# Transposing k and q of ten units by DMA in 16-bit words instead of by TensorE

## The chip, the cores and the metric

The kernel runs on one core of a Trainium2 chip. The metric is the device time of one execution in microseconds, lower being better. The kernel before takes 637.39 us (median of three runs, 636.07 to 639.22). The profile is of one execution with a span of 637.1 us.

## The reference

A linear attention with decay (a "retention") feeds a two-layer network with a SiLU between its layers. Batch 4, 8 heads, 768 positions, head size 64, model width 512, hidden width 2048; all is computed to 32-bit accuracy.

```python
gamma = 1.0 - 2.0 ** (-5.0 - np.arange(H))
for t in range(S):
    state = gamma * state + outer(k[:, :, t], v[:, :, t])     # per batch and head, 64 x 64
    y[:, :, t] = scale * (q[:, :, t] @ state)
x = y.transpose(0, 2, 1, 3).reshape(B * S, H * D)             # 3072 x 512
h = x @ w_in                                                  # 512 -> 2048
g = h * (1.0 / (1.0 + np.exp(-h)))
out = g @ w_out                                               # 2048 -> 512
```

## The kernel before

**Units and visits.** The sequence is cut into 6 chunks of 128 positions. A unit is one chunk of one of the 4 batches, so there are 24 units, numbered chunk by chunk. Inside a chunk the recurrence is written as a masked product of q and k (the scores) plus a product of q with the carried state. A function `visit(m)` advances three units by one stage each: unit m is staged (k and q transposed), unit m - 1 gets its state products and its scores, and unit m - 2 gets its output y.

The scores need k and q with the head dimension on the partitions, but they lie in memory with the position there. `stage_t` (L353) transposes them: four TensorE transposes of 128x128 for k and four for q (L360), each group into one bank of PSUM, and a ScalarE copy of 128x512 for each into the tiles `kt` and `qt` (L362). `stage_s` (L370) uses k untransposed, already scaled by `scale_k` (L330), for the state products; `stage_a` uses `kt` and `qt` for the scores.

**The two layers.** `product_in(c, f)` (L535) is one step of the first layer: chunk c of all four batches (512 rows) by one block f of 128 hidden columns. Each operand is split into a high and a low part, so the step has twelve matmuls of 128x512, eight into the bank `ha` and four into `hb` (L539). ScalarE copies `ha` out (L543), VectorE subtracts `hb` (L547), ScalarE applies SiLU (L551), and one step later SyncE stores the result, g, in DRAM (L557). Three PSUM banks are shared by `ha` and `hb` in turn (`turn`, L317); in the kernel before, the transposed k of a visit takes one turn as well. The tile for g has three buffers. The second layer (L665 on) reads g back and starts near 370 us, when the first is done.

**What sets the order.** The order on TensorE is as written. The main loop (L645) runs through the steps and, behind some of them, a visit: unit 14 behind step (1, 15), units 15 to 17 behind (2, 9), (2, 11), (2, 13), units 18 to 21 behind (3, 1), (3, 5), (3, 9), (3, 13), units 22 and 23 behind (4, 1) and (4, 5). Two further visits, behind (4, 9) and (4, 13), stage nothing and finish the last two units. So visits are two steps apart in chunk 2 and four steps apart later. On the other engines a scheduler orders what is ready, in the order of the program where it can choose. Lists (`behind_copy`, `behind_next`) hold work back until the copy of `ha` or the subtraction of a coming step has been issued.

**Queues.** Nearly all transfers are issued by SyncE, in order: an issue that waits holds up all behind it. Transfers use eight completion semaphores in turn, so an issue may also have to wait for the one eight before it. Loads of k and q for unit m + 2 are issued at the end of visit m (L528), of v for m + 1. Beside them SyncE issues the stores of g, and loads of the weights (`wf`), which VectorE and ScalarE convert from 64-bit words (L172); the converted second-layer weights are stored again (`wod`, L238). The tiles `kf`, `qf` and `vf` have three, two and three buffers.

Of the kernel before, what the change touches and what calls it, by code (L numbers as in the profile page):

```python
# [12 lines left out]
FP32 = mybir.dt.float32  # L13
FP32R = mybir.dt.float32r
U32 = mybir.dt.uint32
AF = mybir.ActivationFunctionType
ALU = mybir.AluOpType

# [13 lines left out]
def kernel(  # L32
# [6 lines left out]
    moe_w_out: bass.AP,  # L39
    out: bass.AP,  # L40
):

# [17 lines left out]
    nc = tc.nc  # L60
    B, H, S, D = q.shape
    DM, DF = moe_w_in.shape
    C = 128
    NC = S // C
    HP = H // 2
# [15 lines left out]
    dram = pool("dram", 1, space=bass.MemoryType.DRAM)  # L81
# [3 lines left out]
    ld = pool("ld", 2)  # L85
    one = pool("one", 1)
# [24 lines left out]
    def split_w(f, w32, name, factor, to):  # L111
# [4 lines left out]
        with tc.issue_after(held[0] if f >= NF - 4 else evac[0]):  # L116
            nc.scalar.activation(out=w[:, 0, :], in_=w32, func=AF.Copy, scale=HALF * factor)
        high = w[:, 0, :].bitcast(FP32)
        yield
        nc.vector.scalar_tensor_tensor(out=lo, in0=w32, scalar=factor, in1=high,  # L120
                                       op0=ALU.mult, op1=ALU.subtract)
        nc.scalar.activation(out=w[:, 1, :], in_=lo, func=AF.Copy, scale=1.0 / EPS)
        nc.vector.scalar_tensor_tensor(out=w[:, 2, :], in0=high, scalar=EPS, in1=lo,
# [3 lines left out]
    units = [(c, b) for c in range(NC) for b in range(B)]  # L127
    kqv = {"k": {}, "q": {}, "v": {}}
    EARLY = 2 * B
    early = {}  # L130

    def load(name, n):
        if n >= len(units):
            return
        c, b = units[n]
        src = {"k": k, "q": q, "v": v}[name]
        if n < EARLY:

            if n not in early:
                early[n] = wpool.tile([128, 3, H, D], FP32, tag=f"w{4 + n}", name=f"kqv_{n}")  # L140
            t = early[n][:, "kqv".index(name)]
        else:
            t = ld.tile([128, H, D], FP32, tag=f"{name}f", name=f"{name}f_{n}",
                        bufs=2 if name == "q" else 3)
        nc.sync.dma_start(out=t, in_=src[b, :, ds(c * C, C)].rearrange("h t d -> t h d"))  # L145
        kqv[name][n] = t
# [6 lines left out]
    def load_w(i):  # L153
        if i >= 2 * NF:
            return
        if wide:
            t = stage.tile([128, 2 * DM], U32, tag="wf", name=f"wf_{i}")
            w_in, w_out, n = moe_w_in.bitcast(U32), moe_w_out.bitcast(U32), 256
        else:
# [12 lines left out]
    def convert_w(i):  # L172
# [130 lines left out]
    xt, kt, qt, am = {}, {}, {}, {}  # L303
    behind_next, behind_mask, behind_copy = [], [], []
# [25 lines left out]
    def scale_k(n):  # L330
        if 0 <= n < len(units):
            t = kqv["k"][n]
            if units[n][0] == NC - 1:
                t = t[:D]
            if 2 * B <= n < 3 * B + 2:

                def half(heads):
                    for h in heads:
                        nc.scalar.activation(out=t[:, h, :], in_=t[:, h, :], func=AF.Copy,
                                             scale=gk[:, units[n][0], h : h + 1])  # L340

                half(range(H // 2))
                behind_copy.append(lambda: half(range(H // 2, H)))
                return
            g = gk[: t.shape[0], units[n][0], :].unsqueeze(2).to_broadcast([t.shape[0], H, D])
            nc.vector.tensor_tensor(out=t, in0=t, in1=g, op=ALU.mult)

    def scale_q(n):
        c, b = units[n]
        t, g = (x if c > 0 else x[:, :, D:] for x in (qt[n], gq))  # L350
        nc.vector.tensor_tensor(out=t, in0=t, in1=g, op=ALU.mult)

    def stage_t(n):  # L353

        for name, to, bufs, src, tp in (
                ("kt", kt, 2, kqv["k"][n], turn(f"kp_{n}")),
                ("qt", qt, 3, kqv["q"].pop(n), banks("q", f"qp_{n}", 1)[:, 0])):
            tp = tp.rearrange("p (a t) -> p a t", a=HP)
            for a in range(HP):
                nc.tensor.transpose(tp[:, a, :], src[:, 2 * a : 2 * a + 2, :], ident)  # L360
            to[n] = one.tile([128, HP, C], FP32, tag=name, name=f"{name}_{n}", bufs=bufs)
            evac[:] = [nc.scalar.copy(out=to[n], in_=tp).ins]  # L362
# [128 lines left out]
    def late_x(b):  # L491
        if b == 0:
            xt[LATE] = xpool.tile([128, 3, KIN, NT], FP32R, tag="xt", name=f"xt_{LATE}")
        with tc.issue_after(copied[0]), tc.issue_after(taken_out[0]):
            split_x(LATE, b, None, y_late.pop(b))

    def visit(m):

        first, mid, last = (0 <= m - i < len(units) for i in range(3))
        if first:  # L500
            stage_t(m)
        if last:
            scores, states_with, yp = stage_y(m - 2)
            scores()
        if mid:
            sc, sums = score_tile(m - 1)
            stage_s(m - 1, sums)
        if last:
            states_with(0)
        if mid:  # L510
            stage_a(m - 1, sc)
            if m > 1 and units[m - 1][1] == 0:
                next_chunk()
            with tc.issue_after(taken_out[0]) if taken_out else ExitStack():
                finish_a(m - 1, sc, sums)
            with tc.issue_after(masked[0]):
                while behind_mask:
                    list(behind_mask.pop(0))
            scale_q(m - 1)
        if m == 0:  # L520
            chunk_decays()
            first_chunk()
        if first:
            scale_k(m)
        if last:
            states_with(1)
            finish_y(m - 2, yp)
        for name, n in (("k", m + 2), ("q", m + 2), ("v", m + 1)):  # L528
            if n >= EARLY:
                load(name, n)  # L530


    pending = []

    def product_in(c, f):  # L535
        ha, hb = turn(f"ha_{c}_{f}"), turn(f"hb_{c}_{f}")
        for i in range(3):
            for kk in range(KIN):
                nc.tensor.matmul(hb if i == 2 else ha, lhsT=w_sb[f][:, i, ts(kk, 128)],  # L539
                                 rhs=xt[c][:, i, kk, :], start=kk == 0 and i != 1,  # L540
                                 stop=kk == KIN - 1 and i != 0)
        hs = hpool.tile([128, NT], FP32, tag="hs", name=f"g_{c}_{f}")
        copied[:] = [nc.scalar.activation(out=hs, in_=ha, func=AF.Copy, scale=ONE_E).ins]  # L543
        with tc.issue_after(copied[0]):
            while behind_copy:
                behind_copy.pop(0)()
        taken_out[:] = [nc.vector.tensor_tensor(out=hs, in0=hs, in1=hb, op=ALU.subtract).ins]  # L547
        with tc.issue_after(taken_out[0]):
            while behind_next:
                behind_next.pop(0)()  # L550
        nc.scalar.activation(out=hs, in_=hs, func=AF.Silu)  # L551
        pending.append((c, f, hs))

    def put_g(keep):
        while len(pending) > keep:
            c, f, g = pending.pop(0)
            nc.sync.dma_start(out=g_dram[c, f], in_=g)  # L557
# [50 lines left out]
    for m in range(EARLY + 2):  # L608
# [9 lines left out]
        elif m == EARLY:  # L618
# [11 lines left out]
    steps = pairs + three + rest + last + groups  # L630
# [6 lines left out]
    at = ([(1, NF - 1)] + [(2, f) for f in range(NF - 7, NF - 2, 2)] +  # L637
          [(c, 4 * i + 1) for c in range(3, NC - 1) for i in range(B)])
# [3 lines left out]
    behind[1, NF - 4] = lambda: [late_x(0), late_y(2), late_x(1), late_y(3)]  # L642
    behind[1, NF - 2] = lambda: late_x(2)
    behind[1, NF - 1] = lambda: [late_x(3), visit(EARLY + 6)]
    for n, (c, f) in enumerate(steps):  # L645
        product_in(c, f)
        if (c, f) in takes:
            take_w(taken_out[0], 2 if n < len(pairs) else int(n < len(pairs + three)))
        put_g(1)
        behind.get((c, f), lambda: None)()  # L650
        if c == NC - 1:
            if f == 0:
                get_w(0)
                get_w(1)
            if f < NF - 4:
                w_out(f)
            if f >= NF - 6:
                if f == NF - 6:
                    for n in range(G_AHEAD):
                        get(n)  # L660
                if f >= NF - S_AHEAD:
                    split(f - NF + S_AHEAD)
    put_g(0)

    for c in range(NC):  # L665
# [8 lines left out]
        for f in range(NF):  # L674
            n = c * NF + f
# [3 lines left out]
            t = ready.pop(n)  # L679
# [9 lines left out]
        for b in range(B):  # L689
            oa, ob = acc[b]  # L690
            o = one.tile([128, DM], FP32, tag=("kt", "qt")[b % 2], name=f"o_{c}_{b}",
                         bufs=(2, 3)[b % 2])
            rows = ds(b * S + c * C, C)
# [7 lines left out]
            n = 2 if b == B - 1 else 1  # L701
# [36 lines left out]
```

## Time and profile before

| | |
|---|---|
| time, median of 3 | 637.39 us |
| TensorE busy, matmuls | 613.2 us (96%) |
| VectorE busy | 421.7 us (66%) |
| ScalarE busy | 305.7 us (48%) |
| TensorE transposes of units 8 to 23 | 64 of k and 64 of q, 272 ns each, overlapping |
| ScalarE copies of them, all units | 48, 0.58 us each |
| loads of q for units 8 to 23 | 16 of 256 KB, 4.4 us from issue to landing |
| loads of k for units 8 to 23 | 16 of 256 KB, 5.2 us from issue to landing |
| moved by DMA | 103.65 MB, of which 80016 packets under 512 bytes |

Matmuls are pipelined: the durations of single ones overlap, so the cost of a group is read from the start of its first to the start of what follows. The chain of waits follows the work that ended last back through the execution; where it lists one group of TensorE after another without a wait, TensorE alone sets the time. The time to landing of a transfer runs from its issue to the completion that a waiting engine sees.

### The profile page before, as it was taken

How to read it: one execution, taken by the hardware profiler on the slowest of the kernel's cores; microseconds unless marked ns; L12 is line 12 of the kernel's file. 1: busy time of each engine (PE TensorE's matmuls, PEld its weight loads, DVE VectorE, ACT ScalarE, POOL GpSimd, SP SyncE). 2: the span in 40 equal slices, each digit the busy share in tenths (PEclk: the TensorE clock that was granted, in tenths of full speed). 3: DMA queues.
4: the chain of work that ended last, by engine and by line, in shares of the span. 5: the costliest groups of instructions: out<-in, count | busy, mean ns of one | idle time of the engine just before them, and what ended most of it. 6: DMA issues, size and time to landing. Idle time of an engine off the chain costs nothing.

```text
span 637.1 us, 13560 instructions
## 1 busy us (share of the span) xinstructions
PE 613.2 (96%) x5440; PEld 509.1 (80%) x5440; DVE 421.7 (66%) x731; ACT 305.7 (48%) x590; POOL 7.5 (1%) x65
## 2 busy tenths in 40 slices
PE   5787999999999999999999999999999999999997
PEld 3676878888888888888878888888888888888785
DVE  2896798789977778687878675463644544554631
ACT  5576897676756555555467861231412221312311
POOL 3000000000000000000000000000000000000000
PEclk9987999999999999999999999999999999999999
DMA  9985877455677687874657644242432524342301
GB/s 200 208 207 119 218 219 227 167 175 175 204 224 191 189 224 214 229 228 171 219 184 242 199 150 124 81 163 94 137 128 84 181 68 131 132 129 85 117 0 67
DMA packets 123215, 103.65 MB, mean 163 GB/s; under 512 B 80016, under 2 KB 88464, under 8 KB 123152
## 3 DMA queue, kind: packets, MB, share of 16 engines
q1 hardware_dynamic: 120272, 97.54, 53.1%
q10 hardware_dynamic: 2880, 5.24, 2.2%
q8 instruction: 43, 0.70, 0.5%
q14 instruction: 20, 0.16, 0.1%
HBM read 66.06 MB, written 36.70 MB: 161 GB/s over the span
## 4 chain that ended last, share of the span: by engine, by line
PE 90%; SPq 3%; DVE 2%; ACT 1%; issue 1%; DMA 1%; DVEq 0%; ACTq 0%; POOLq 0%
PE ha L539 28%; PE o L687 20%; PE hb L539 13%; PE oa L687 13%; PE ob L687 7%; PE y L419 3%; SPq L145 3%; PE sc L386 1%; PE sc L376 1%; PE kp L360 1%; PE qp L360 1%; DMA kqv<-in_q_dram 1%; SPq L167 0%; DVE o L696 0%; SPq L165 0%
## 5 line engine op out<-in xcount | busy, mean ns | idle before, releaser
L539 PE MATMUL ha<-xt,wi 128*128 128x512 f32 x768 | 195.0, 396 | 1.9 <-ACT xt L466 1.9
L539 PEld LDWEIGHTS ha<-xt,wi 128*128 128x128 f32 x768 | 144.2, 190 | 32.9 <-ACT xt L466 2.0
L687 PE MATMUL o<-wo,gs 128*128 128x512 f32 x576 | 146.2, 389 | 0.0
L687 PEld LDWEIGHTS o<-wo,gs 128*128 128x128 f32 x576 | 108.1, 188 | 22.4
L596 DVE TENSOR_TENSOR gs<-gr,gs 128x512 fp32r<-128x512 f32 x96 | 62.1, 686 | 90.7 <-ACT gs L594 90.7
L687 PE MATMUL oa<-wo,gs 128*128 128x512 f32 x384 | 118.3, 389 | 0.0
L594 ACT ACTIVATE gs<-gr 128x512 fp32r<-128x512 f32 x96 | 53.4, 621 | 134.7 <-issue 132.3
L539 PE MATMUL hb<-xt,wi 128*128 128x512 f32 x384 | 103.5, 392 | 0.0
L547 DVE TENSOR_TENSOR g<-g,hb 128x512 f32<-128x512 f32 x96 | 65.7, 684 | 45.4 <-ACT g L543 26.2
L539 PEld LDWEIGHTS hb<-xt,wi 128*128 128x128 f32 x384 | 72.9, 190 | 15.5
L551 ACT ACTIVATE g<-g 128x512 f32<-128x512 f32 x96 | 60.7, 632 | 48.7 <-DVE g L547 48.4
L687 PEld LDWEIGHTS oa<-wo,gs 128*128 128x128 f32 x384 | 72.1, 188 | 14.9
L687 PE MATMUL ob<-wo,gs 128*128 128x512 f32 x192 | 75.2, 392 | 0.3 <-DVE o L696 0.3
L543 ACT ACTIVATE g<-ha 128x512 f32<-128x512 f32 x96 | 56.8, 591 | 36.0 <-PE ha L539 27.4
L597 DVE SCALAR_TENSOR_TENSOR gs<-gs 128x512 fp32r<-128x512 f32 x96 | 62.0, 684 | 0.0
L687 PEld LDWEIGHTS ob<-wo,gs 128*128 128x128 f32 x192 | 36.0, 188 | 9.3 <-DVE o L696 2.0
L193 ACT ACTIVATE ca<-wf 128x512 f32<-128x512 f32 x32 | 21.6, 674 | 9.2 <-DVE cs L200 4.9
L394 DVE TENSOR_TENSOR am<-sc,decay 128x512 f32<-128x512 f32 x24 | 16.5, 687 | 11.5 <-PE sc L386 11.5
L419 PE MATMUL y<-qt,mid 64*64 64x64 f32 x384 | 22.6, 233 | 1.3 <-issue 1.3
L200 DVE SCALAR_TENSOR_TENSOR cs<-ca,cs 128x512 uint32<-128x512 uint32 x32 | 22.1, 691 | 1.0
L204 DVE SCALAR_TENSOR_TENSOR cp<-wf,cp 128x512 f32<-128x512 uint32 x32 | 22.1, 690 | 0.7
L695 ACT ACTIVATE o<-o 128x512 f32<-128x512 f32 x10 | 6.0, 598 | 33.4 <-PE o L687 33.0
(79 smaller groups left out, 543.2 us busy)
## 6 DMA issues: line engine op xcount, KB each, us to landing
gd<-g SPq DMA_DIRECT2D x96, 256.0 KB, 3.1
gr<-gd SPq DMA_DIRECT2D x96, 256.0 KB, 2.7
wf<-in_moe_w_out_dram SPq DMA_DIRECT2D x16, 512.0 KB, 4.4
out_dram<-o ACTq DMA_DIRECT2D x20, 256.0 KB, 2.1
wf<-in_moe_w_in_dram SPq DMA_DIRECT2D x16, 256.0 KB, 3.3
wf<-in_moe_w_in_dram SPq DMA_DIRECT2D x32, 128.0 KB, 3.8
kf<-in_k_dram SPq DMA_DIRECT2D x16, 256.0 KB, 5.2
qf<-in_q_dram SPq DMA_DIRECT2D x16, 256.0 KB, 4.4
```

The lines of the kernel that those rows point to most:

```text
L193: nc.scalar.activation(out=a.bitcast(FP32), in_=hi.bitcast(FP32), func=AF.Abs, scale=65536.0)
L200: nc.vector.scalar_tensor_tensor(out=s, in0=a, scalar=3, in1=s, op0=ALU.logical_shift_left, op1=ALU.bitwise_or)
L204: nc.vector.scalar_tensor_tensor(out=p.bitcast(FP32), in0=lo, scalar=2.0 ** -52, in1=p.bitcast(FP32), op0=ALU.mult, op1=ALU.mult)
L419: i = nc.tensor.matmul(yp[ts(e, D), o, a, :], lhsT=lhsT, rhs=rhs, start=(e, o) not in started, stop=True, skip_group_check=True).ins
L539: nc.tensor.matmul(hb if i == 2 else ha, lhsT=w_sb[f][:, i, ts(kk, 128)], rhs=xt[c][:, i, kk, :], start=kk == 0 and i != 1, stop=kk == KIN ...
L543: copied[:] = [nc.scalar.activation(out=hs, in_=ha, func=AF.Copy, scale=ONE_E).ins]
L547: taken_out[:] = [nc.vector.tensor_tensor(out=hs, in0=hs, in1=hb, op=ALU.subtract).ins]
L551: nc.scalar.activation(out=hs, in_=hs, func=AF.Silu)
L594: nc.scalar.activation(out=t[:, 0, :], in_=g, func=AF.Copy, scale=HALF)
L596: nc.vector.tensor_tensor(out=t[:, 1, :], in0=g, in1=high, op=ALU.subtract)
L597: nc.vector.scalar_tensor_tensor(out=t[:, 2, :], in0=t[:, 1, :].bitcast(FP32), scalar=-1.0 / EPS, in1=high, op0=ALU.mult, op1=ALU.add)
L687: nc.tensor.matmul(o, lhsT=g, rhs=wo[f][:, i, :], start=first_ and i != 1, stop=last and i != 0)
```

## The change

For units 14 to 23 (`FAR` is 14) TensorE no longer transposes k and q. Four transfers and two copies take its place:

- `gather_t`: k and q of the unit are copied inside DRAM, from eight heads' rows into one row of 2 KB for each position.
- `fetch_t`: that copy, seen as 16-bit words, is transposed on its way into SBUF by a DMA transpose: 128 positions by 1024 words, so that partition p holds word p of each head, low and high halves of the 32-bit numbers on alternate partitions.
- `order_t`: four transfers for each of k and q sort the partitions, low halves and high halves each into a plane of its own, even heads on the lower 64 partitions and odd heads on the upper.
- `join_t`: one ScalarE copy for each interleaves the two planes, word by word, into the 32-bit tiles `qt` and `kt`.

The main loop puts the gather four steps ahead of the unit's step, the transpose one step ahead, the sorting into the step itself (ahead of its visit) and the joining one step after. k is still needed untransposed, for the state products; it is now loaded at the end of the unit's own visit rather than two visits ahead, and scaled one step later where visits are two steps apart, two steps later otherwise. q isn't loaded in its old form any more. The transposed words use the buffers of `qf`, the planes those of `kf`. The purpose is to free TensorE, the busiest engine, of work that needs no arithmetic.

```diff
+    FAR = 3 * B + 2
...
+    def gather_t(n):
+        c, b = units[n]
+        for name, src in (("q", q), ("k", k)):
+            t = dram.tile([128, H, D], FP32, tag=f"{name}{n}", name=f"{name}d_{n}")
+            nc.sync.dma_start(out=t, in_=src[b, :, ds(c * C, C)].rearrange("h t d -> t h d"))
+            rows[name, n] = t
+    def fetch_t(n):
+        for name in "qk":
+            t = ld.tile([128, H, C], U16, tag="qf", name=f"{name}w_{n}", bufs=2)
+            nc.sync.dma_start_transpose(
+                out=t, in_=rows.pop((name, n)).bitcast(U16).rearrange("t h w -> t (h w)"))
+            words[name, n] = t
+    def order_t(n):
+        for name in "qk":
+            src = words.pop((name, n)).rearrange("p (a j) t -> p j a t", j=2)
+            t = ld.tile([128, 2, HP, C], U16, tag="kf", name=f"{name}p_{n}", bufs=3)
+            for w in range(2):
+                for j in range(2):
+                    nc.sync.dma_start(out=t[ts(j, D), w], in_=src[w::2, j])
+            planes[name, n] = t
+    def join_t(n):
+        for name, to, bufs in (("q", qt, 3), ("k", kt, 2)):
+            to[n] = one.tile([128, HP, C], FP32, tag=f"{name}t", name=f"{name}t_{n}", bufs=bufs)
+            nc.scalar.copy(out=to[n].bitcast(U16).rearrange("p a (t w) -> p w a t", w=2),
+                           in_=planes.pop((name, n)))
...
-        if first:
+        if first and m < FAR:
             stage_t(m)
...
-        if first:
+        if first and m < FAR:
             scale_k(m)
...
-            if n >= EARLY:
+            if n >= EARLY and (n < FAR or name == "v"):
                 load(name, n)
+        if m >= FAR:
+            load("k", m)
...
+    far = {steps.index(x): EARLY + 6 + i for i, x in enumerate(at) if EARLY + 6 + i < len(units)}
     for n, (c, f) in enumerate(steps):
+        if n - 1 in far:
+            behind_copy.append(lambda m=far[n - 1]: join_t(m))
+            if n + 1 in far:
+                behind_next.append(lambda m=far[n - 1]: scale_k(m))
+        elif n - 2 in far and n not in far:
+            behind_next.append(lambda m=far[n - 2]: scale_k(m))
         product_in(c, f)
...
         put_g(1)
+        if n in far:
+            order_t(far[n])
+        if n + 1 in far:
+            fetch_t(far[n + 1])
+        if n + 4 in far:
+            gather_t(far[n + 4])
         behind.get((c, f), lambda: None)()
```

More of the change, by code (lines that the diff above doesn't have):

```diff
@@ L15 @@
 U32 = mybir.dt.uint32
+U16 = mybir.dt.uint16
 AF = mybir.ActivationFunctionType
@@ L351, in scale_q @@
         nc.vector.tensor_tensor(out=t, in0=t, in1=g, op=ALU.mult)
+    rows, words, planes = {}, {}, {}
+    def gather_t(n):
[23 more added lines that the diff above has]
+                           in_=planes.pop((name, n)))
     def stage_t(n):
```

## The prediction

> **What bounds the kernel now.** I read the busy times, then the slices, then the chain of waits in order of time.
>
> ```profile
> PE 613.2 (96%) x5440; PEld 509.1 (80%) x5440; DVE 421.7 (66%) x731; ACT 305.7 (48%) x590; POOL 7.5 (1%) x65
> ...
> PE   5787999999999999999999999999999999999997
> ...
> DMA  9985877455677687874657644242432524342301
> ```
>
> TensorE is busy in nine tenths or more of every slice from about 95 us on, so one microsecond of its work in that stretch is one microsecond of the span, provided that nothing else then makes it wait. Units 14 to 23 are visited between 180 and 295 us, inside it. There the transfers are the next busiest resource: the row of stretches gives a DMA share of 0.72 and a PE without a gap.
>
> ```profile
> 216.00:300.00 84.00, 84.00 (x1056) 70.92 (x1055) 62.06 (x112) 44.07 (x79) 0.53 (x6) 1.00 0.72 214
> ```
>
> The chain shows what a visit costs. Each line is the eight ha matmuls of one step; a step without a visit is 2.72 us (289.31 less 286.59).
>
> ```profile
> 286.59 1.81 PE ha L539 x8
> 289.31 1.81 PE ha L539 x8
> 294.99 2.04 PE ha L539 x8
> ...
> 303.39 1.81 PE ha L539 x8
> 308.19 2.04 PE ha L539 x8
> ```
>
> The visit of unit 23 lies between 289.31 and 294.99 (5.68 us), the visit after it, which stages no unit and so transposes nothing, between 303.39 and 308.19 (4.80 us). Both do the smaller state products of the last chunk. The eight transposes therefore cost TensorE **0.88 us a visit**. The timeline of the visit of unit 17 agrees to a tenth: from the first transpose to the first y matmul it is 0.97 us.
>
> ```profile
> 207.44 0.60 PE L360 MATMUL kp<-ident,kf 128*128 128x128 f32 x4
> 207.88 0.60 PE L360 MATMUL qp<-ident,qf 128*128 128x128 f32 x4
> 208.41 0.69 PE L419 MATMUL y<-am,vf 64*64 64x64 f32 x32
> 208.93 0.65 PE L376 MATMUL sc<-vf,kf 64*64 64x64 f32 x32
> ```
>
> **What the Trainium skill says.** "VectorE: DVE Perf Modes", The three transpose paths, prices one 128x128 16-bit transpose at 390 ns on TensorE and 1309 ns by DMA. The trace's 32-bit transpose takes 272 ns, and eight overlap into 0.88 us, so the first figure is not what counts here; no DMA transpose is in the trace. "DMA: Bandwidth & Descriptors", Latency and other measured facts, gives 261 GB/s for a DMA transpose, measured on one kernel. The two prices differ by ten if tiles do not run side by side, and are my bounds. The same page, Anatomy of one DMA, says that transfer engines do not wait on semaphores: the wait sits on the issuing sequencer. The trace agrees: SyncE waits 60.1 us between 150 and 310 us for the activations whose result it is to store, everything behind them waiting too.
>
> **The change, part by part.**
>
> Removed: 10 visits x 0.88 = **8.8 us** of TensorE. Also twenty evacuations of 0.58 us on ScalarE, and ten q loads.
>
> Added on ScalarE: twenty joins of 128x1024 16-bit words. Copies in the trace:
>
> ```profile
> L362 ACT COPY kt<-kp 128x512 f32<-128x512 f32 x24 | 14.0, 582 | 7.1 <-PE kp L360 6.9
> L401 ACT COPY mid<-sc 128x256 f32<-128x256 f32 x4 | 1.5, 369 | 3.3 <-DVE am L394 3.3
> ```
>
> (582 - 369) / 256 = 0.83 ns an element, so 1024 take 582 + 512 x 0.83 = 1.01 us: 0.86 us more a visit. ScalarE is busy 44 of 84 us in that stretch, so the work alone costs nothing. A strided write could be slower; at twice the price it is still inside the idle time.
>
> Added transfers. Nearest rows:
>
> ```profile
> gr<-gd SPq DMA_DIRECT2D x96, 256.0 KB, 2.7
> ...
> wf<-in_moe_w_in_dram SPq DMA_DIRECT2D x32, 128.0 KB, 3.8
> kf<-in_k_dram SPq DMA_DIRECT2D x16, 256.0 KB, 5.2
> ```
>
> Twenty gathers of 256 KB inside DRAM. In the order as built they are issued ahead of unit 14's visit, up to 100 us early, among loads and stores that have slack; I cost them at nothing, hidden by the matmuls (the DMA share there is 0.5 to 0.8).
>
> Twenty transposes of 256 KB. Bounds: 256 KB at 261 GB/s is 1.0 us; eight tiles one after another at 1.31 us are 10.5 us. I take 1 us of moving and a landing of 3 to 4 us, between the gr and the kf row, since whole tiles should spread over the engines as loads do.
>
> Eighty 64 KB plane copies, at 3.8 us to landing (the wf half loads, also 64 partitions) and about 0.33 us of issue each, so 2.6 us of SyncE a unit.
>
> Per unit the last two kinds add 1024 KB and q's load drops out: 768 KB in the 14 us of four steps and a visit, 56 GB/s on the 211 GB/s of 175 to 300 us. The stretch of 178 to 186 us already runs at 256 GB/s with a share of 0.81, so the sum is tight but not above what was seen by much.
>
> Added waits. The plane copies wait for the transpose; stores of g, weight loads and the k load queue behind them on SyncE. The join waits for the planes; the next evacuations of ha queue behind it on ScalarE, and TensorE waits for their banks. With visits four steps apart (units 18 to 23), counted from the start S of the visit's step: the transposes go out at about S - 1, behind the store of two steps back; landed by S + 3, planes out by S + 5.5, landed by S + 9.5. The next step starts at S + 4.8, its ha is copied by S + 7.4, and the q join stands behind that. TensorE needs the following ha bank at S + 12.05 (4.8 + 2 x 2.72 + 1.81), so with a 0.63 us activation and a 0.6 us copy between, the join must end by S + 10.8. It ends at about S + 10.5. The k join is a step later in the built order, with more slack. These six visits I cost at nothing, with half a microsecond to spare.
>
> Visits two steps apart (units 15 to 17) do not fit so well. Before, k came two visits early; now it is loaded at the end of its own visit, behind the eight plane copies. In the built order, k of unit 16 is scaled on VectorE behind the subtraction of step (2, 13) and behind the rest of a weight conversion. Before, those ran at:
>
> ```profile
> 208.77 0.68 DVE L547 TENSOR_TENSOR g<-g,hb 128x512 f32<-128x512 f32 x1
> 209.37 0.42 DVE L202 TENSOR_SCALAR cp<-cs 128x512 uint32<-128x512 uint32 x1
> ...
> 210.31 0.69 DVE L204 SCALAR_TENSOR_TENSOR cp<-wf,cp 128x512 f32<-128x512 uint32 x1
> 211.03 0.69 DVE L210 TENSOR_TENSOR cw<-cs,cp 128x512 f32<-128x512 f32 x1
> ```
>
> The scaling (0.68 us) now follows: it would end near 212. But unit 17's visit, starting at 207.44, needs that k for its state products 0.5 us in (208.93 - 207.44 less the 0.97 us of transposes). TensorE waits at most 4.3 us; at least 2.5 us even if VectorE is idle before (0.1 + 0.6 + 0.34 + 0.6 + 0.7 + 0.68 - 0.5). I take 3.5. Unit 16's visit meets the same for k of unit 15 by up to 0.8 us (take 0.5). Unit 17's own transposes are issued behind a weight store that waits for that conversion, and the store of step (2, 13), whose buffer step (3, 0) reuses, is behind its planes: nothing lost if a transpose lands in 3 us, 3.7 us if in 5; I take 1.
>
> Sum: -8.8 + 3.5 + 0.5 + 1 = **-3.8 us, 633.6 us**.
>
> **Rivals.**
> (a) Only the forced 2.5 us is lost: 637.4 - 8.8 + 2.5 = 631.1. For it: TensorE's neighbours idle often. Against it: k really is late by the queue's order. (Nothing lost at all would be 628.6.)
> (b) A transpose lands like a k load (5 us): unit 17 costs 3.7 and six later units about 0.5 each in late joins: -8.8 + 4.3 + 0.8 + 3.7 + 3 = +3, 640.4 us. For it: 256-byte pieces make k loads slow today, and the DMA share is already 0.72.
> (c) Half the tile-by-tile price: 5.2 us of moving and 2 of latency. q lands at S + 6.5, k at S + 11.5 behind it, its planes at S + 16.3, the k join ends at S + 17.3 against a deadline of S + 13.5: 3.8 us a unit for eight units is 30, so 637.4 - 8.8 + 30 = 659. At the full price k lands at S + 22.5 and the join ends 13.5 us late: 8 x 13.5 - 8.8 = +99, 737 us. Against it: the other price. For it: the trace of before cannot exclude it. This is the case that ends **slower**, with the join on ScalarE the new bound.
>
> **How the numbers follow.** Forecast 633.6: 0.45 (0.35 of it faster by over 0.5%, below 634.2; 0.10 within). (a) 0.12. (b) 0.15, half within 0.5%, half slower. (c) up to 660: 0.18; up to 737: 0.10. Faster 0.47, within 0.17, slower 0.36. The range leaves out the far end of (c) and the unhindered gain: 630 to 660.
>
> **What would show it.** Steps (3, 5) to (4, 5) with a visit at 4.9 to 5.0 us instead of 5.68 would confirm the removal; a gap in TensorE inside the visit of unit 17, released by VectorE's scaling of k, the late load. A copy of qt or kt on ScalarE that waits for plane transfers by several microseconds, with ha following it, is (c). The transposes' time to landing decides: 3 to 4 us supports the forecast, 7 or more refutes it. Unmoved stretches before 175 us and after 300 us would show the gathers to be free.

## The result, and the profile after

The changed kernel takes **671.88 us** (median of 4 runs, 671.56 to 673.57) against 638.20 us before on the same chip: a ratio of 1.054, with a 95% interval of 1.050 to 1.057. The prediction, 633.6 us with a range of 630 to 660, missed it by 38 us, on the wrong side.

The busy times and TensorE's slices on the page of the changed kernel:

```profile
PE 614.7 (92%) x5360; PEld 504.5 (75%) x5360; DVE 422.4 (63%) x731; ACT 319.4 (48%) x590; POOL 7.2 (1%) x65
...
PE   5778989999996896977989999999999999999997
```

The matmuls are 80 fewer (5440 to 5360), as meant. But the row of TensorE, which before held a 9 from the fifth slice to the last but one, now has holes between slices 13 and 20, from about 200 to 335 us: there the visits lie, from that of unit 16 on. Outside the stretch of the visits nothing moved by more than 2 us (step (2, 8) starts 1.5 us later than before, and from the start of step (5, 0) to the end the two kernels differ by 0.1 us). The row of stretches for the one that the prediction showed:

```profile
216.00:300.00 84.00, 70.58 (x788) 56.49 (x780) 48.58 (x87) 41.17 (x61) 0.44 (x5) 0.92 0.86 202
```

TensorE is busy 70.58 of 84 us there (84.00 before); the transfers' share went from 0.72 to 0.86, but the rate fell, from 214 to 202 GB/s. No other engine is near its limit. The waits between 170 and 330 us, each line with the sum, the number and the longest, say who stands for whom:

```profile
PEld hb L580 <- ACT g L584: 21.2, 7, 7.3
...
DVE kf L350 <- DMA kf<-in_k_dram: 14.6, 5, 5.4
ACT g L584 <- DMA gd<-g: 14.4, 6, 4.1
...
ACT qt L389 <- DMA qp<-qw: 12.0, 7, 2.9
```

TensorE stands for ScalarE, which has not copied `ha` out of its bank (L584). ScalarE in turn stands for two kinds of transfer: the store of an earlier g, whose buffer the copy needs (14.4 us; 3.5 in the same stretch before), and the planes of q, at the join (12.0 us). VectorE waits for k (14.6 us). What these three kinds of transfer all share is the queue they are in: SyncE's. (The planes and k also share three buffers, to which I come back at the end.) The chain of waits, in order of time, runs through the same stations:

```profile
253.68 1.20 PE hb L580 x4
...
257.43 2.60 DMA qp<-qw
260.12 1.37 ACT qt L389
...
262.51 5.29 DMA gd<-g
267.90 0.60 ACT g L584
```

TensorE's second half of a step (hb), planes of q and the join, a store of g, and the copy of ha that waited for it. Over the whole run TensorE is 59% of this chain, 90% before. SyncE's timeline (start, duration, what it issued) at that place:

```profile
249.52 2.59 SPq L371 DMA_TRANSPOSE qw<-qd  x1
252.16 2.02 SPq L371 DMA_TRANSPOSE kw<-kd  x1
...
255.40 2.65 SPq L382 DMA_DIRECT2D qp<-qw  x4
258.09 2.59 SPq L382 DMA_DIRECT2D kp<-kw  x4
...
262.51 2.14 SPq L598 DMA_DIRECT2D gd<-g  x3
```

From 249.5 to 264.6 us it issues without a pause (the left-out lines are stores and loads of 0.4 to 0.5 us each, among them the k load and a weight load and store behind the plane copies). The three stores of g at the end have gathered behind the plane copies, and ScalarE's next copy of `ha` waits until 267.90 for one of them to land. The durations of an issue, shortest, median and longest in ns, by tile:

```profile
L382 SPq DMA_DIRECT2D qp<-qw x40: 593/618/2572, 93.8 to 329.9; - x40
L371 SPq DMA_TRANSPOSE qw<-qd x10: 1357/1800/2592, 87.9 to 321.8; - x10
```

and the rows of the joins and the transfers' landings that answer to those of before:

```profile
L389 ACT COPY qt<-qp 128x1024 uint16<-128x1024 uint16 x10 | 13.5, 1354 | 15.1 <-DMA qp<-qw 14.1 <-DMA kp<-kw 1.0
...
qp<-qw SPq DMA_DIRECT2D x40, 64.0 KB, 3.2
...
qw<-qd SPq DMA_TRANSPOSE x10, 5.6
```

For k the copies land in 2.6 us and the transposes in 4.6.

The measure used below is the length of a step with a visit, from the start of its first ha matmul to that of the next step (us; a step without a visit is mostly 2.72 in each):

| step, unit | before | changed | copies left out | idle copies on SyncE |
|---|---|---|---|---|
| (2, 9), 15 | 5.77 | 4.90 | 4.90 | 5.77 |
| (2, 11), 16 | 5.77 | 6.81 | 4.90 | 5.77 |
| (2, 13), 17 | 5.77 | 10.92 | 5.56 | 5.81 |
| (3, 1), 18 | 5.77 | 9.71 | 5.70 | 5.80 |
| (3, 5), 19 | 5.77 | 5.99 | 4.90 | 8.00 |
| (3, 9), 20 | 5.77 | 13.75 | 4.90 | 7.48 |
| (3, 13), 21 | 5.77 | 5.47 | 4.90 | 10.06 |
| (4, 1), 22 | 5.77 | 14.50 | 4.89 | 5.97 |
| (4, 5), 23 | 5.77 | 4.89 | 4.89 | 6.41 |

The last two columns are `x_nosort` and `x_dummy` below. And the time that SyncE spends issuing transfers (the durations of the issues added up, waits for semaphores not counted) from the start of step (3, 0) to that of (4, 10): 32.6 us of 92.1 before, **90.0 us of 115.8** in the changed kernel.

### The profile page after: what moved, and what is told of

Same layout as the page of the kernel before. It is cut to its first block, busy times and chain, and to the rows that moved or that the text cites. A ratio compares the mean times of both kernels' runs of the same rounds, so it can differ in the third digit from the quotient of the medians.

```text
span 669.8 us, 13526 instructions
## 1 busy us (share of the span) xinstructions
PE 614.7 (92%) x5360; PEld 504.5 (75%) x5360; DVE 422.4 (63%) x731; ACT 319.4 (48%) x590; POOL 7.2 (1%) x65
## 2 busy tenths in 40 slices
DMA packets 176496, 116.77 MB, mean 174 GB/s; under 512 B 133296, under 2 KB 141744, under 8 KB 176432
## 4 chain that ended last, share of the span: by engine, by line
PE 59%; DMA 14%; DVE 9%; ACT 8%; SPq 5%; issue 4%; ACTq 0%; DVEq 0%; POOLq 0%
PE o L742 19%; PE oa L742 13%; PE ha L580 12%; PE ob L742 7%; PE hb L580 7%; DMA gd<-g 4%; DMA qw<-qd 3%; SPq L382 2%; DMA qp<-qw 2%; SPq L149 2%; DMA wf<-in_moe_w_in_dram 2%; ACT g L584 2%; DVE g L588 1%; DMA yd<-ys 1%; DMA kf<-in_k_dram 1%
## 5 line engine op out<-in xcount | busy, mean ns | idle before, releaser
L580 PE MATMUL hb<-xt,wi 128*128 128x512 f32 x384 | 106.8, 401 | 21.8 <-ACT g L584 21.8
L584 ACT ACTIVATE g<-ha 128x512 f32<-128x512 f32 x96 | 56.6, 590 | 49.9 <-PE ha L580 20.8
```

## The experiments

Each run was timed against the kernel before on the same chip; times are medians, ratios have their 95% interval. The expectations give letters to the theories: A, SyncE's time; B, the movement of the data, slowed by the new transfers; C, the wait of a weight store that stands among the plane copies; D, a ring of waits through the stores of g; E, planes that are late at the join.

| run | us | ratio to before |
|---|---|---|
| x_ideal: plain loads for transposes, no copies | 632.20 | 0.989 (0.985 to 0.994) |
| x_nosort: plane copies left out | 636.08 | 0.995 (0.993 to 0.996) |
| x_plain: plain loads for transposes | 667.88 | 1.048 (1.042 to 1.053) |
| x_onecopy: one copy for four | 654.31 | 1.024 (1.019 to 1.029) |
| x_takes: conversions moved | 672.17 | 1.055 (1.051 to 1.058) |
| x_pool: copies issued by GpSimd | 665.65 | 1.044 (1.037 to 1.051) |
| x_gdact: g stores issued by ScalarE | 672.23 | 1.050 (1.045 to 1.055) |
| x_before_gdact: the same in the kernel before | 640.70 | 1.004 (1.002 to 1.005) |
| x_far18: units 18 to 23 alone | 659.12 | 1.033 (1.030 to 1.037) |
| x_late18: and joins one step later | 651.88 | 1.023 (1.019 to 1.026) |
| x_lead18: x_far18, transfers earlier | 656.90 | 1.029 (1.025 to 1.033) |
| x_lead18p: and copies by GpSimd | 654.53 | 1.027 (1.024 to 1.031) |
| x_lead18f: and clear of the fences | 647.62 | 1.015 (1.011 to 1.019) |
| x_lead18fg: and gathers by GpSimd | 651.40 | 1.019 (1.014 to 1.024) |
| x_lead18f2: x_lead18f, more lead | 647.51 | 1.013 (1.009 to 1.018) |
| x_lead18_gdact: x_lead18, g stores by ScalarE | 652.48 | 1.023 (1.017 to 1.029) |
| x_dummy: before, and idle copies on SyncE | 655.98 | 1.026 (1.024 to 1.029) |
| x_dummy_pool: the same copies by GpSimd | 641.84 | 1.004 (1.001 to 1.006) |

### Which of the added parts costs it

**The plane copies left out.**

```diff
-            src = words.pop((name, n)).rearrange("p (a j) t -> p j a t", j=2)
-            t = ld.tile([128, 2, HP, C], U16, tag="kf", name=f"{name}p_{n}", bufs=3)
-            for w in range(2):
-                for j in range(2):
-                    nc.sync.dma_start(out=t[ts(j, D), w], in_=src[w::2, j])
-            planes[name, n] = t
+            planes[name, n] = words.pop((name, n)).rearrange("p (w a) t -> p w a t", w=2)
```

> The eighty plane copies are left out (the joins read the transposed words unsorted, scaled by a quarter to keep them finite, so the scores use other data). Theory A, SyncE's queue is the bound: 8 x 0.65 = 5.2 us of issue a unit go, and the stores of g are no longer behind them; most of the 27 us lost in the stretch of units 16 to 23 comes back, 640 us or less. Theory B, the engines that move the data are slowed by the transposes themselves: the transposes stay, so the stores of g stay slow (4 to 5 us to land) and the time stays above 655. Theory C, the wait for the weight store between the plane copies: this too falls away, so C expects about what A does, 640 to 645.

(In this run and in `x_plain`, `x_ideal` and `x_onecopy` the join also scales by a quarter.) 636.08 us: 35.8 us less than the changed kernel, as A expected. With gathers, transposes, joins and the late k all in place, seven of the nine visits of the table are back to 4.9 us. Its row of stretches:

```profile
216.00:300.00 84.00, 82.06 (x1018) 67.30 (x1018) 65.02 (x119) 52.73 (x82) 0.54 (x6) 1.00 0.95 245
```

The DMA engines are busier (0.95) and faster (245 GB/s) than in the changed kernel, and TensorE hardly notices. Full transfer engines alone are not what holds it.

**The transposes replaced by plain loads of the same size, copies kept.**

```diff
-            nc.sync.dma_start_transpose(
-                out=t, in_=rows.pop((name, n)).bitcast(U16).rearrange("t h w -> t (h w)"))
+            nc.sync.dma_start(
+                out=t.rearrange("t h w -> t (h w)"),
+                in_=rows.pop((name, n)).bitcast(U16).rearrange("t h w -> t (h w)"))
```

> Each DMA transpose is replaced by a plain load of the same 256 KB into the same tile (so the scores use other data); the plane copies stay. Theory A: the issue falls from about 4 us to under 1 us a unit and the landing from 5.3 to about 3 us, but the 5.2 us of plane copies stay: about half of the loss comes back, 648 to 658. Theory B: all the loss that the transposes cause by moving comes back, 640 or less. Theory C: the weight store still stands between the copies: 660 or more.

667.88 us, 4.0 less than the changed kernel. That is outside what A expected (648 to 658) and in C's range, which `x_takes` below rules out. A was wrong about the sum: SyncE's issuing from step (3, 0) to (4, 10) falls from 90.0 us to 73.0 of 113.0, and hardly anything is gained; what stays are the eight copies in a row and the hop through a second tile. With both edits together:

> Both the transposes (replaced by plain loads of the same size) and the plane copies are left out; gathers, late k loads and joins stay, so the scores use other data. It measures what the removal on TensorE is worth when nothing stands in its way: all theories 629 to 634, the 8.8 us of transposes less what the late k loads and the gathers cost.

632.20 us: what the removal from TensorE is worth when nothing stands in its way. Between this and `x_nosort` the transposes cost 3.9 us, the same as with the copies. So transposes cost about 4 us, hardly more than the intervals can tell, and the copies about 36.

### Is it an order of waits, or SyncE's time?

**The weight conversions moved,** because a weight store that waits for VectorE stands among the plane copies.

```diff
-    takes += [(c, f) for c in (3, 4) for f in (0, 3, 6, 8, 11, 14)]
+    takes += [(c, f) for c in (3, 4) for f in (2, 3, 6, 10, 11, 14)]
```

> Nothing is left out: in chunks 3 and 4 the weight conversions go behind steps 2, 3, 6, 10, 11, 14 instead of 0, 3, 6, 8, 11, 14, so that none falls just ahead of a visit. Theory C: the visits behind (3,1), (3,9), (4,1), which now lose 4 to 9 us each, lose about what those behind (3,5) and (3,13) do, and (4,9) nothing: 648 to 652. Theory A: SyncE has as much to issue as ever, so the loss moves to other steps: 665 to 672. Theory B: 668 to 672.

672.17 us: nothing gained, against the 648 to 652 of C. That store is not the cause.

**The stores of g in a queue of their own,** and the same edit in the kernel before, as its price.

```diff
-            nc.sync.dma_start(out=g_dram[c, f], in_=g)
+            nc.scalar.dma_start(out=g_dram[c, f], in_=g)
```

> Nothing is left out: the stores of g are issued by ScalarE, which makes g, instead of SyncE; the plane copies, transposes and weights stay on SyncE. Theory D, a ring of waits in SyncE's one queue (plane copies wait for transposes and for a weight store, the stores of g wait behind them, ScalarE's next copy waits for a buffer of g, and the conversion that the weight store waits for comes after it): the ring is cut, 633 to 645, and no wait of ScalarE for a store of g over 1 us. Theory E, the planes themselves are late at the join, whatever else is in the queue: ScalarE still stands at the joins, 655 or more.

> The control for the run above: the kernel before with the stores of g on ScalarE's queue. ScalarE is half idle, so 635 to 641 under every theory; were it well below that, the gain above would not be a cure of the change's own loss.

672.23 us, and 640.70 for the control, some 2 us over before. The waits for g stores go, and the same time comes back elsewhere; waits of `x_gdact`, 170 to 330 us:

```profile
ACT qt L389 <- DMA qp<-qw: 8.5, 3, 3.7
...
PE sc L415 <- DVE kf L350: 7.2, 2, 5.5
ACT kt L389 <- DMA kp<-kw: 6.6, 5, 4.2
```

So the ring through the g stores is one route, not the cause: with it closed, late planes and a late k take the same time.

**One straight copy in place of four,** which leaves the words unsorted.

```diff
-            for w in range(2):
-                for j in range(2):
-                    nc.sync.dma_start(out=t[ts(j, D), w], in_=src[w::2, j])
+            nc.sync.dma_start(out=t.rearrange("p w a t -> p (w a t)"),
+                              in_=src.rearrange("p h t -> p (h t)"))
```

> The four plane copies of 64 KB with 256-byte pieces are replaced by one straight copy of the same 256 KB (so the words are not sorted and the scores use other data; the joins scale by a quarter to keep them finite). Two issues a unit instead of eight; the hop through a second tile, and its wait for the transpose, stays. Theory A, issue time: 4 us a unit come back, 640 or less. Theory D: the queue is shorter but the wait for the transpose still stands ahead of the stores of g: 640 to 650. Theory E: the hop is as late as before: 655 or more.

654.31 us, between the ranges of D and E and in none of the three. Two copies a unit in place of eight, of about 0.5 us of issue each, and half of the 36 us is gone. The small pieces are gone too (111856 packets under 512 bytes, 133296 in the changed kernel), so this run does not part them from the time to issue. The other half stays, with the second hop itself: from the tile of the transposed words to another. SyncE's own waits ahead of the copies, 170 to 330 us:

```profile
SPq L380 <- ACT qt L388: 7.5, 3, 2.8
SPq L380 <- DMA kw<-kd: 6.7, 3, 4.2
```

So a copy stands not for its transpose alone, but as long for a join on ScalarE; in the program that join reads the planes of the unit before, out of the buffer that the copy is to write.

**The copies issued by GpSimd.**

```diff
-                    nc.sync.dma_start(out=t[ts(j, D), w], in_=src[w::2, j])
+                    nc.gpsimd.dma_start(out=t[ts(j, D), w], in_=src[w::2, j])
```

> Nothing is left out: the eighty plane copies are issued by GpSimd, which is idle, instead of SyncE. Theory A: SyncE loses 5.2 us of issue a unit and the head-of-line wait for the transposes; 640 to 648, with the stores of g landing in about 3 us of their readiness. Theory B: the same bytes move, 668 to 672. Theory C: the weight store no longer stands between the copies, 645 to 650, with the four steps (3,1), (3,9), (4,1), (4,9) gaining most.

665.65 us, in none of the three ranges, and inconclusive. Four of the long steps return to 4.9 us: (3, 1), (3, 9), (4, 1) and (4, 9). But the small memsets (`token`, L330) by which the program orders TensorE's accumulations are on GpSimd too, and now stand behind copies that wait, for transposes and for ScalarE; over the whole run:

```profile
PE y L458 <- POOL token L330: 21.0, 7, 6.4
```

A queue of its own was confounded with a new wait of up to 6.4 us.

**SyncE's time alone.** The kernel before, with transfers of the plane copies' size and count that wait for nothing and for which nobody waits, kept in their place behind the g store of the step (`far` and `stored` are set in lines not shown). SyncE's list of waits has none ahead of them.

```diff
         put_g(1)
+        if n in far:
+            with tc.issue_after(stored[0]):
+                src = decay.rearrange("p j a d -> p (j a) d")
+                for i in range(8):
+                    t = dram.tile([D, 4, D], FP32, tag=f"du{n}_{i}", name=f"du_{n}_{i}")
+                    nc.sync.dma_start(out=t, in_=src[ts(i % 2, D), i // 2 % 2::2])
```

> The kernel before, with eight further transfers of 64 KB (64 partitions, four pieces of 256 bytes) issued by SyncE in the step of each of units 14 to 23, where the changed kernel issues its plane copies. They read a table that never changes, write to DRAM that nobody reads, wait for nothing and nobody waits for them. So only their time on SyncE and their bytes are added. Theory A (SyncE's time alone): 645 to 670. Theory E and the in-order waits (the copies hurt because they wait, and are waited for): 636 to 642. Theory B (bytes and pieces): some tenths of the loss, and transfers that land later than before.

655.98 us: **17.7 us slower than before, for transfers that wait for nothing and that nobody uses.** SyncE's timeline at the first loss, step (2, 15), which takes 8.13 us:

```profile
202.23 5.79 SPq L658 DMA_DIRECT2D du<-decay  x8
...
212.31 1.89 SPq L559 DMA_DIRECT2D gd<-g  x2
214.25 5.25 SPq L658 DMA_DIRECT2D du<-decay  x8
```

and ScalarE's, with the idle time and its releaser in brackets:

```profile
218.35 1.22 ACT L543 ACTIVATE g<-ha 128x512 f32<-128x512 f32 x2 [7.56 <-DMA gd<-g]
```

Two stores of g come out at 212.3 behind the transfers and loads of the visit before, and ScalarE stands 7.56 us for their landing. The first of the two had been ready since 200.4. The waits, 170 to 330 us:

```profile
ACT g L543 <- DMA gd<-g: 28.0, 10, 7.6
```

28.0 us against 3.5 before, and TensorE's loads of hb stand for that copy. Why so little is enough can be worked out from the trace: g has three buffers, so one comes round every 3 x 2.72 = 8.16 us. From the copy of `ha` to the end of the last activation are 2.1 us (255.40 to 257.47 in the changed kernel), and a store lands 3.6 us after its issue (3.1 before). That leaves 8.2 - 2.1 - 3.6 = 2.5 us for a store to wait in the queue (an estimate; 3.0 with the landing of before; a visit in between adds its own 2 to 3 us). Eight copies take 5.25 (the line above).

**The same transfers by GpSimd:** `nc.gpsimd` for `nc.sync` in the last line, and the last memset in GpSimd's order in place of the store, so that they go out up to one visit earlier.

> x_dummy with the eight idle transfers of a unit issued by GpSimd, behind the last memset of the visit before, in place of SyncE: the same bytes, pieces and count, without a microsecond of SyncE's time. Theory A: within 2 us of the kernel before, 636 to 641. Theory B (the bytes and small pieces slow the other transfers): 648 to 658, as x_dummy.

641.84 us, 2.4 us over before and just above the 636 to 641 of theory A. The bytes are the same. But the profile records them in other packets (number, MB, share of the DMA engines' time):

```profile
q0 software_dynamic: 2560, 5.25, 3.0%
```

In `x_dummy` they are 21760 packets more than before, of 256 bytes for the most part. So the time of this run does not by itself clear the small pieces. The stores of g do. From the end of the activation that makes a g to the issue of its store, steps (2, 8) to (4, 12), are 0.64 us on average in the kernel before, **3.24 us in `x_dummy`**, 0.81 here; from issue to landing 3.40, 3.97 (23 of the 37 landings recorded) and 4.23. The stores land slowest where hardly anything is lost; what `x_dummy` has more of is standing in the queue. Most of the other fifteen microseconds are SyncE's time.

### Can the loss be designed away?

If lead or another queue removes it, there is a version that beats both. These runs take the DMA way for units 18 to 23 alone, whose visits are four steps apart.

```diff
-    FAR = 3 * B + 2
+    FAR = 4 * B + 2
...
-    far = {steps.index(x): EARLY + 6 + i for i, x in enumerate(at) if EARLY + 6 + i < len(units)}
+    far = {steps.index(x): EARLY + 6 + i for i, x in enumerate(at) if FAR <= EARLY + 6 + i < len(units)}
```

> The way by DMA for units 18 to 23 alone (FAR is 18), the units whose visits are four steps apart, nothing else changed. In the changed kernel the stretch from step (3, 2) to (4, 11) lost 21 us net of the removed transposes. Theory A (SyncE's time: a unit adds about 10 us of issuing, for 14 us in a period of 13 us) and theory E (the planes are late at the join because copies follow a transfer that must land first) both say that these six units lose by themselves: 650 to 662. If instead the loss was a backlog that units 15 to 17 (two steps apart) left in the queue, these six are free: 633 to 636.

659.12 us: six units alone lose 21 us, so it is no mere backlog of units 15 to 17.

**Joins later:**

```diff
-        if n - 1 in far:
-            behind_copy.append(lambda m=far[n - 1]: join_t(m))
+        if n - 2 in far:
+            behind_copy.append(lambda m=far[n - 2]: join_t(m))
```

> x_far18 with each join one step later (two steps after the unit's step in place of one); no transfer moves. Theory E: only the join stood in the way, its deadline is now 2.7 us later, so most of the loss of x_far18 goes: 632 to 642. Theory A: k loads, weight stores and g stores are as late as before, and TensorE waits for them instead: within 5 us of x_far18.

651.88 us, 7.2 less than `x_far18`: between the two expectations. The join's deadline is a real part, about a third.

**Transfers earlier:**

```diff
-        if n in far:
-            order_t(far[n])
-        if n + 1 in far:
-            fetch_t(far[n + 1])
-        if n + 4 in far:
-            gather_t(far[n + 4])
+        if n + 1 in far:
+            order_t(far[n + 1])
+        if n + 3 in far:
+            fetch_t(far[n + 3])
+        if n + 7 in far:
+            gather_t(far[n + 7])
```

> x_far18 with the transfers earlier: gathers seven steps ahead of the unit's step, transposes three, plane copies one step ahead; joins as in x_far18. The number of issues and bytes is the same. Theory E: the planes have landed at the join, 632 to 640. Theory A: the queue has as much to issue in each period of four steps, so nearly all of the loss stays, 645 to 660, as waits of the g stores and k loads.

656.90 us, 2.2 less. Lead on the same queue buys almost nothing: the queue has as much to issue as ever. That is the forecast of theory A (645 to 660).

**And the copies by GpSimd,** first plainly (`nc.gpsimd` for `nc.sync` in `order_t`), then each behind the last memset (`fenced`) of the visit before:

> x_lead18 with the plane copies issued by GpSimd, whose queue holds nothing else but two small memsets at the end of each visit. Takes 5 us of issuing a unit off SyncE as well as giving lead. Theories A and E both: 631 to 636, faster than x_lead18 by most of what that one still loses; if it still loses ten microseconds or more, neither the lead nor SyncE's time is the cause, but the movement of the data itself.

```diff
-                    nc.sync.dma_start(out=t[ts(j, D), w], in_=src[w::2, j])
+                    with tc.issue_after(fenced[0]):
+                        nc.gpsimd.dma_start(out=t[ts(j, D), w], in_=src[w::2, j])
```

> x_lead18p, with each plane copy put behind the last memset of the visit before (in GpSimd's order of issue), so that no memset that TensorE waits for stands behind a copy that waits for a transpose. In x_lead18p TensorE waited 23 us for those memsets, 7 us of it in chunk 2. If they were the rest of the loss: 632 to 637. If SyncE's in-order waits for the transposes' issue are: 645 or more.

654.53 and 647.62 us. By the expectation's own words the first would have ruled out both the lead and SyncE's time; but TensorE waited there for the memsets, a wait that the edit itself brought in. Clear of them, 7 us more are gone, and still 9 us are lost against the 632 to 637 hoped for. The gathers by GpSimd too:

> x_lead18f with the gathers issued by GpSimd too. SyncE keeps the transposes (1.3 to 2.0 us each), which is about 2.5 us more a unit than the q load it loses. Theory A: as x_lead18f or up to 3 us faster. If the gathers' landing through GpSimd's queue is much slower, the transposes wait for them on SyncE, and it is slower than x_lead18f.

651.40 us (647.2 to 654.0): not better, perhaps worse. One more step of lead, transposes four steps ahead (three for unit 18), copies two:

> x_lead18f with one more step of lead: gathers eight, transposes four (three for unit 18), plane copies on GpSimd two steps ahead. In x_lead18f GpSimd waited 26 us for transposes, and TensorE 17 us for memsets behind the copies. If the lead removes those waits: 633 to 639. If the transposes' own issue on SyncE (3 us a unit) is enough to delay the g stores: 642 or more.

647.51 us: TensorE no longer waits for a memset, and the time is the same. Its waits, 170 to 330 us:

```profile
ACT g L587 <- DMA gd<-g: 21.5, 8, 5.6
...
DVE kf L352 <- DMA kf<-in_k_dram: 12.2, 4, 4.8
```

The copies are off SyncE, but the transposes (1.5 and 1.9 us of issue on average) are still on it, and now wait there for the copies to free their buffers (11 us in all), with the g stores behind them. The copies in turn wait on GpSimd for ScalarE's joins to free theirs:

```profile
POOL qp L385 <- ACT qt L392: 22.2, 4, 7.3
```

So buffers limit the lead here: words have two, planes and k three between them. No run gives them more.

**Two routes closed at once:** `x_lead18` with the g stores on ScalarE's queue.

> x_lead18 with the stores of g issued by ScalarE, in a queue of their own. In x_dummy most of TensorE's stalls follow a g store that is late in SyncE's queue (28 us of waits of the copy of ha for a store), and in the run with g stores on ScalarE alone the joins stood instead. If these two are the routes by which SyncE's time reaches TensorE, the planes' lead and the stores' own queue together remove the loss: 634 to 640 (g stores on ScalarE cost 2.3 us in the kernel before, six visits give 5.3). If other waits in SyncE's queue (weights, k loads) are routes of their own: 645 or more.

652.48 us: a third route opens. Its waits:

```profile
DVE cw L214 <- DMA wod<-cw: 12.4, 4, 5.3
...
ACT ca L197 <- DMA wf<-in_moe_w_out_dram: 11.0, 3, 4.5
```

Weights, for whose stores VectorE waited 1.8 us in the kernel before, now come late from the same queue. No version that sorts the words is faster than the kernel before; the two runs that are leave the sorting out.

## Why the prediction was wrong, by its own steps

**The removal** was right: an unhindered visit is 4.90 us in place of 5.77, 0.87 us less. `x_ideal` shows what arrives of the forecast 8.8 us: about 7.

**The joins** take 1.35 us rather than 1.01 (the prediction allowed up to twice), and cost nothing by themselves: `x_nosort` and `x_ideal` have them. **The gathers** were rightly free, in the same runs.

**The transposes** were the step I thought would decide. They land in 4.6 and 5.6 us (medians), as in rival (b), not 3 to 4 and not the 7 that was to refute the forecast, and cost 4 us. What I gave no number at all is their issue: 1.8 and 2.1 us of SyncE each. The fear of rival (c), tiles one after another, did not come true; its time of 659 was the nearest. Its sign did appear, joins that wait for planes with ha following (12.0 us), but not from slow transposes, so the time was near by luck.

**The plane copies** are the step that failed, twice. As a term it was mis-sized: 0.62 us of issue, not 0.33, so 5.0 us of SyncE a unit, and with the transposes 9. ("Four transfers" in the list of the change are kinds: a unit has twelve issues, of which eight are plane copies.) And it was set against the wrong limit. I added up bytes, 56 GB/s on 211, and found room. `x_nosort` moved 245 GB/s without harm; whether 267 would have fitted is not shown, for the changed kernel never got there (202). I never added up SyncE: 32.6 us of 92 used, and 6 units x 9 us to come. The prediction even counted "2.6 us of SyncE a unit" and "stores of g ... queue behind them", and then, for these six units, asked only whether the joins meet their deadline. The stores' own slack of 2.5 to 3 us could have been worked out from the same trace.

**"Six visits at nothing, with half a microsecond to spare"** cost 25 us net from step (3, 0) to (4, 11). A margin of half a microsecond at the end of a chain of six estimated terms was no margin: the issue of the copies, the landing of the transposes and the join were each longer, and the queue ran late (the planes of unit 19, whose visit starts on TensorE at 249.06, go out at 255.40).

**The late k** of units 15 to 17 had the right mechanism. Around the visit of unit 17 in the changed kernel, VectorE's and then TensorE's timeline:

```profile
213.86 0.69 DVE L350 TENSOR_TENSOR kf<-kf,gk 128x512 f32<-128x512 f32 x1 [0.97 <-DMA kf<-in_k_dram]
```

```profile
214.61 1.13 PE L415 MATMUL sc<-vf,kf 64*64 64x64 f32 x32 [4.65 <-DVE kf L350]
```

4.65 us where I took 3.5 with an upper bound of 4.3; 0.97 of it VectorE stood for the load itself. But it is not a cost of the late load as such: without the copies the loads leave in time, the built order scales k ahead of the conversion, and the same step loses 0.66 us; my "at least 2.5" was too much.

**How the 36 us divide** is settled only roughly. SyncE's time alone gives 17.7 us (`x_dummy`), the second hop with almost no issuing of its own 18.2 (`x_onecopy` less `x_nosort`). That the two make up the whole may be chance, since they feed each other: what waits holds the queue, and a full queue makes what waits later. Shown is that the loss needs the copies, that idle transfers in SyncE's order cost half of it, that the same bytes issued elsewhere cost 2 us, and that closing one route alone (g stores, conversions, lead) gave some 2 us at most, later joins 7. Not settled is how much of the second half is the wait on the queue, how much the planes' lateness at the join, and how much the buffers that planes, words and k take from each other: leaving the copies out frees those too, and no run gave them buffers of their own. Copies off SyncE still lose (`x_pool`, and `x_lead18f2` by 8 us), so its time is not the whole. Nor do I know why issues of plain loads sometimes take over 1 us, which they do in the kernel before too.

## What to carry to other kernels

Ahead of adding transfers, add up the issuing engine as an engine of its own: number of transfers by the duration of an issue, per period, against what it already issues; and for everything behind them in the queue work out how long it can stand (buffers times period, less work, less landing). A burst longer than the shortest such slack can be paid for even where the sum has room: ten bursts of 5 us cost 17.7 us here with SyncE issuing 65.0 us of 103.1, while 17 us less issuing of transposes (`x_plain`) gave 4. Closing the route that the waits name helps little while other transfers stand in the same queue. And a second hop needs buffers as well as issues.

## What was unexpected in the hardware

- An issue of a 64 KB copy from SBUF to SBUF (64 partitions, four pieces of 256 bytes) takes 0.62 us of SyncE (0.59 the shortest), as long as a whole 256 KB load of k (0.57, median before), and so does one of the same shape from SBUF to DRAM. The Trainium skill, "DMA: Bandwidth & Descriptors", Issuing engines are not separate DMA queues, says that issuing on several engines saves only the initiating time, "usually small relative to the DMA itself". Here it is 0.62 us beside 2.6 to 3.2 us to landing, and eight in a row are not small. "Perfetto Trace Analysis", What "DMA-bound" means, names the issuing sequencer as a bound of its own, when its track is solid with DMA issues; the 90.0 of 115.8 us agree, but the 17.7 us of `x_dummy` were lost at 65.0 of 103.1, so it need not be solid.
- A DMA transpose of 256 KB occupies SyncE for 1.2 to 2.6 us, and lands in 4.6 to 5.6 us.
- A ScalarE copy with 16-bit words interleaved on the write takes 1.35 us for 1024 elements a partition, where the slope of the 32-bit copies gave 1.01.
